# Attention with a threshold, then a token and channel mixer: fewer weight conversions in two units, and a second layer for two tiles in turn

## The chip, the cores and the metric

The kernel runs on one core of one Trainium2 chip. The metric is device time in microseconds (us). The kernel before took 1351.52 us in the median of three runs, from 1350.7 to 1352.07. The engines of the core are named as in the profile: PE is TensorE (matrix multiplications; PEld are its weight loads), DVE is VectorE, ACT is ScalarE, POOL is GpSimd, and SP is SyncE, which here only starts transfers. A name with q behind it (SPq, ACTq) is the queue in which that engine issues its transfers.

## The reference

For 8 batches of 8 heads, 576 tokens and 64 values a head, each row of scores is cut at a threshold below its maximum, and what is left goes through a softmax. The heads are then put side by side to 512 channels, and a mixer follows: two layers over the tokens (576 to 256 to 576) with a sum, and two layers over the channels (512 to 1536 to 512) with a sum.

```python
scores = scale * np.matmul(q, k.transpose(0, 1, 3, 2))
thresh = np.max(scores, axis=-1, keepdims=True) - tau
scores = np.where(scores >= thresh, scores, -1000000000.0)
scores = scores - np.max(scores, axis=-1, keepdims=True)
attn = np.exp(scores)
attn = attn / (np.sum(attn, axis=-1, keepdims=True) + 1e-09)
attn_out = np.matmul(attn, v)
# ... heads side by side: x is (8, 576, 512)
h = np.maximum(xt @ w_tok1, 0.0) @ w_tok2       # xt: x with tokens last
u = x + h.transpose(0, 2, 1)
h2 = np.maximum(u @ w_ch1, 0.0) @ w_ch2
return u + h2
```

The four weight matrices come as 64-bit floating-point numbers. [...] the kernel takes them apart as integer words and puts 32-bit numbers together: this is what is called conversion below.

## The kernel before

The program is one loop over 144 *units*. A unit is 128 rows of scores for the two heads of a pair; 18 units are one batch, called a row here (units 0 to 17 are row 0, units 18 to 35 are row 1). The instructions of each engine run in the order in which the loop writes them down.

Softmax of a unit: TensorE computes the scores of both heads into two banks, VectorE takes the row maxima, GpSimd makes the bias from them, ScalarE subtracts, cuts and exponentiates, GpSimd divides by the sums. From row 1 on two banks serve all units, so the scores of a unit wait until ScalarE's first activation (`Prelu`) has read those of the unit before.

```python
def scores(u):
    # ...
    nc.tensor.matmul(sc[h][rows, f, 0:HS], lhsT=qT[r, cols], rhs=kT[r, HS * f : HS * f + HS], start=True, stop=True)
    # ...
    nc.vector.tensor_reduce(out=mx[:, c], in_=sc[h][:, :, 0:HS], axis=AX.XY, op=ALU.max)
    nc.gpsimd.tensor_scalar(out=bias[:, c], in0=mx[:, c], scalar1=toff, scalar2=-SCALE, op0=ALU.add, op1=ALU.mult)

def weigh(u):
    # ...
    nc.scalar.activation(out=eh, in_=sc[h][:, :, 0:HS], func=AF.Prelu, bias=bias[:, h : h + 1], scale=SCALE, alpha=STEEP)
    # ...
    nc.scalar.activation(out=eh, in_=eh, func=AF.Exp, bias=ntau, accum_out=rs[:, h : h + 1])
```

Two units later the weights are transposed (*turned*) for the product with the values. In row 0 this is done on TensorE, into two banks that VectorE and ScalarE empty in turn (`turn`). From row 1 on it is done in 32 by 32 blocks on VectorE, and every third unit SyncE issues 16 transfers that put the blocks in place (`turn_blocks`). The first two units of row 1, 18 and 19, still turn the last two units of row 0.

```python
def turn(u, third):
    # ...
    on = nc.scalar.copy if third == 1 else nc.vector.tensor_copy
    on(out=eTs[key][:, 3 * third : 3 * third + 3, P * place : P * place + P], in_=ps)

def turn_blocks(u):
    # ...
    nc.vector.transpose(
        out=T[:, :, place, :].rearrange("p a (c x) -> p c a x", c=NK), in_=e.rearrange("p (c a x) -> p c a x", c=NK, a=4)
    )
    if place == GU - 1:
        # ...
        for a in range(4):
            for i in range(4):
                nc.sync.dma_start(out=eT[32 * a : 32 * a + 32, :, i, :], in_=T[32 * i : 32 * i + 32, a, :, :])
```

The conversion: 31 pieces (0 to 2 and 3 to 6 for the two token layers, 7 to 18 for the first channel layer, 19 to 30 for the second), three steps each, and step number k is part k mod 3 of piece k div 3. Part 0 lets GpSimd finish the piece before and then loads a raw piece three ahead into one of four raw buffers, in SyncE's queue; parts 1 and 2 are ScalarE's two operations on the *next* piece; every part has one of VectorE's three operations. `need` runs all steps up to one that a matmul needs.

```python
def weight(n):
    for k in range(steps_done, min(steps_done + n, 3 * len(pieces) + 1)):
        i, part = divmod(k, 3)
        if part == 0:
            on_gpsimd(i - 1)
            if i:
                load_piece(i - 1 + NRAW)
        else:
            on_scalar(i + 1, part - 1)
        on_vector(i, part)
        steps_done = k + 1

def need(i):
    weight(3 * i + 4 - steps_done)
```

The mixer's matmuls are steps in a list, `todo`, each with a cost. `fill` takes them from it and places them between the units. For a group of 256 tokens, the first channel layer is 12 steps (`ch1`), and the second, for each of two tiles of 128 tokens, four parts of three matmuls that sum into one bank (`ch2`). The pool `ps_mm` has two banks.

```python
def ch2(t, part):
    need(7 + NJ + 3 * part + 2)
    # ...
    if part == 0:
        s["ps"] = ps_mm.tile([P, NCC, P], F32, tag="mm", name=f"c2_{b}_{i}_{t}")
    ps = s["ps"]
    # ... three matmuls into ps; after part 3 the bank goes to SBUF and out
```

The loop, cut to the order of its parts (`turns_left` holds in units 18 and 19 alone):

```python
turns_left = b_now and back and not in_blocks(units[w][0])
scores(u)
# ... values of row 0
norm(u - 1)
if b_now:
    if turns_left:
        weigh(u)
    else:
        weight(2)
# ... copies; turns on TensorE
if b_now:
    fill(0.4)
if back and in_blocks(wb):
    turn_blocks(w)
if b_now:
    weight(4 if turns_left else 2)
if turns_left:
    fill(0.6)
elif on and (b_now or not visit):
    weigh(u)
# ...
if b_now:
    weight(2)
# ... loads and block transposes of q and k for later pairs; values
```

Of the kernel before, what the change touches and what calls it, by code (L numbers as in the profile page):

```python
# [9 lines left out]
F32 = mybir.dt.float32  # L10
# [7 lines left out]
P = 128  # L18
# [3 lines left out]
def kernel(  # L22
# [38 lines left out]
    NCC = DM // P  # L61
# [16 lines left out]
    ps_mm = None  # L78
# [98 lines left out]
    def load_piece(i):  # L177
        if i >= len(pieces):
            return
        dst, src = pieces[i]  # L180
        rows = dst.shape[0]
        n = 1
        for d in dst.shape[1:]:
            n *= d
        raw = raw_at[i % NRAW][0:rows, 0 : n * (2 if wide(i) else 1)].bitcast(src.dtype)
        nc.sync.dma_start(out=like(raw, dst), in_=src)
        if wide(i):
            words = raw.bitcast(U32).rearrange("p (n w) -> p n w", w=2)
            h2 = high[0:rows, WMAX * (i % 2) : WMAX * (i % 2) + n]
            raws[i] = like(words[:, :, 0], dst), like(words[:, :, 1], dst), like(h2, dst)  # L190
        else:
            raws[i] = like(raw, dst)
# [4 lines left out]
    def on_scalar(i, part):  # L197
        if wide(i):
            lo, hi, h2 = raws[i]
            if part == 0:  # L200
                nc.scalar.activation(out=lo.bitcast(I32), in_=lo, func=AF.Copy, scale=2.0**-29)
            else:
                nc.scalar.activation(out=h2, in_=hi.bitcast(F32), func=AF.Abs)
# [17 lines left out]
    def on_gpsimd(i):  # L221
        if i >= 0:
            dst = pieces[i][0]
            if wide(i):
                nc.gpsimd.tensor_tensor(out=dst.bitcast(I32), in0=dst.bitcast(I32), in1=raws.pop(i)[0].bitcast(I32), op=ALU.add)
            else:
                nc.gpsimd.tensor_copy(out=dst, in_=raws.pop(i))
# [5 lines left out]
    def weight(n):  # L233

        nonlocal steps_done
# [10 lines that stand above are left out]
# [5 lines left out]
    def need(i):  # L251

        weight(3 * i + 4 - steps_done)
# [27 lines left out]
    def in_blocks(b):  # L281
        return b > 0
# [201 lines left out]
    def channel_mlp(b, uT, i):  # L484

        s = {}
        n = min(GR, 2 * S - GR * i)
        nt = n // P

        def turn_u():  # L490

            us, ut = s["us"], s["ut"]
            nc.vector.transpose(
                out=us[:, 0:nt].rearrange("q n a (c d) -> q c (n a) d", c=NCC),
                in_=uT[:, :, GR * i : GR * i + n].rearrange("q c (m r) -> q c m r", r=32),
            )

            def move(a, k):
                nc.sync.dma_start(out=ut[32 * a : 32 * a + 32, 0:nt, k, :], in_=us[32 * k : 32 * k + 32, 0:nt, a, :])

            moves.extend([lambda a=a, k=k: move(a, k) for a in range(4) for k in range(4)])

        def ch1(j):
            need(7 + j)
            if j == 0:
                s["g"] = work.tile([P, NJ, GR], F32, tag="g", bufs=1, name=f"g_{b}_{i}")
            ps = ps_mm.tile([P, GR], F32, tag="mm", name=f"c1_{b}_{i}_{j}")[:, 0:n]
            for c in range(NCC):
                nc.tensor.matmul(ps, lhsT=wc1[:, j, c, :], rhs=uT[:, c, GR * i : GR * i + n], start=(c == 0), stop=(c == NCC - 1))  # L509
            nc.scalar.activation(out=s["g"][:, j, 0:n], in_=ps, func=AF.Relu)  # L510
            if j == 1:
                s["us"] = work.tile([P, GR // P, 4, NCC * 32], F32, tag="us", bufs=1, name=f"us_{b}_{i}")
                if b:
                    s["ut"] = work.tile([P, GR // P, 4, NCC * 32], F32, tag="ut", bufs=1, name=f"ut_{b}_{i}")
                    turn_u()

        def ch2(t, part):
            need(7 + NJ + 3 * part + 2)
            t0 = GR * i + P * t
            if part == 0:  # L520
                s["ps"] = ps_mm.tile([P, NCC, P], F32, tag="mm", name=f"c2_{b}_{i}_{t}")
            ps = s["ps"]
            flat = ps.rearrange("q c d -> q (c d)")
            if part == 0 and not b:
                for c in range(NCC):
                    nc.tensor.matmul(
                        ps[:, c, :], lhsT=uT[:, c, t0 : t0 + P], rhs=ident, is_transpose=True, start=(c == 0), stop=False, skip_group_check=True
                    )
            for j in range(3 * part, 3 * part + 3):
                nc.tensor.matmul(  # L530
                    flat,
                    lhsT=s["g"][:, j, P * t : P * t + P],
                    rhs=wc2[:, j, :],
                    start=(j == 0 and b > 0),
                    stop=(j == NJ - 1),
                    skip_group_check=True,
                )
            if part == 3:
                o = s["us"][:, t].rearrange("q a x -> q (a x)")
                if b:  # L540
                    move_u()
                    nc.vector.tensor_add(  # L542
                        out=o.rearrange("q (c k d) -> q c k d", c=NCC, k=4),
                        in0=ps.rearrange("q c (k d) -> q c k d", k=4),
                        in1=s["ut"][:, t].rearrange("q k (c d) -> q c k d", c=NCC),
                    )
                else:
                    nc.vector.tensor_copy(out=o, in_=flat)
                nc.sync.dma_start(out=out[b : b + 2].rearrange("b s d -> (b s) d")[t0 : t0 + P, :], in_=o)

        def ch2_last(half):

            t0 = GR * i
            w = DM // 2
            ps = ps_mm.tile([P, w], F32, tag="mm", name=f"c2_{b}_{i}_h{half}")
            for j in range(NJ):
                nc.tensor.matmul(  # L557
                    ps, lhsT=s["g"][:, j, 0:P], rhs=wc2[:, j, w * half : w * half + w], start=(j == 0), stop=(j == NJ - 1)
                )
            if half == 0:  # L560
                move_u()
            o = s["us"][:, half].rearrange("q a x -> q (a x)")[:, 0:w]
            cs = slice(NCC // 2 * half, NCC // 2 * half + NCC // 2)
            nc.vector.tensor_add(
                out=o.rearrange("q (c k d) -> q c k d", c=NCC // 2, k=4),
                in0=ps.rearrange("q (c k d) -> q c k d", c=NCC // 2, k=4),
                in1=s["ut"][:, 0].rearrange("q k (c d) -> q c k d", c=NCC)[:, cs],
            )
            nc.sync.dma_start(out=out[b : b + 2].rearrange("b s d -> (b s) d")[t0 : t0 + P, w * half : w * half + w], in_=o)

        if b == B - 2 and n == P:
            return [(0.0067 * n, lambda j=j: ch1(j)) for j in range(NJ)] + [(5.2, lambda half=half: ch2_last(half)) for half in range(2)]
        return [(0.0067 * n, lambda j=j: ch1(j)) for j in range(NJ)] + [
            (2.6 if part or b else 3.0, lambda t=t, part=part: ch2(t, part)) for t in range(nt) for part in range(4)
        ]

    def move_u():
        while moves:
            moves.popleft()()
# [56 lines left out]
    def values_due(u):  # L636
        while due and due[0][0] <= u:
            _, b, p0, g = due.popleft()
            values(b, p0, g)
            if b == 0 and p0 == 0 and g == 2:  # L640
                return True
            if p0 == NP - 2 and g == 2:
                if not in_blocks(b):
                    return True
                push(b)
        return False

    for u in range(len(units) + LAG + 4):
        on = u < len(units)
        if u == UB:  # L650
            late.close()
            ps_mm = ctx.enter_context(tc.tile_pool(name="ps_mm", bufs=2, space=bass.MemoryType.PSUM))
        if on:
            b_now, p0, t = units[u]
# [6 lines left out]
        last = False  # L661
        visit = False
        if due and not in_blocks(due[0][1]):
            visit = due[0][0] <= u
            last = values_due(u)
# [6 lines left out]
        turns_left = b_now and back and not in_blocks(units[w][0])  # L672
# [29 lines left out]
        if back and in_blocks(wb):  # L702
            turn_blocks(w)
        if b_now:
            weight(4 if turns_left else 2)
        if turns_left:
            fill(0.6)
        elif on and (b_now or not visit):
# [62 lines left out]
```

## Time and profile before

| what | before |
| --- | --- |
| median of three runs | 1351.52 us (1350.7 to 1352.07) |
| span of the profiled run | 1349.9 us |
| busy: PE, DVE, ACT, POOL | 1306.6, 592.2, 585.1, 352.5 us |
| chain that ended last, PE's share | 86% |
| chain, DVE's share and that of transfers | 6% and 3% |
| one maximum on DVE (L311) | 750 ns |
| one block transpose on DVE (L369) | 1364 ns |
| one first activation on ACT (L321) | 739 ns |
| raw weight load (512 KB), issue to landing | 3.7 us |

The rows of the page are groups of instructions with the same line of the program: L306 scores, L311 maxima, L312 bias, L321 and L328 the activations, L357 and L359 the turns of row 0 and the copies out of their banks, L369 the block transposes and L378 their transfers, L201 and L203 ScalarE's conversion operations, L211, L213 and L217 those of VectorE, L225 that of GpSimd, L186 the raw loads, L413 and L418 the products with the values, L425 the copies of these, L456 and L466 the token layers, L470 the sums behind them, L509 and L510 the first channel layer, L526 and L530 the second. The chain of waits is the work that ended last, followed back from the end: what is not in it did not set the time. The slices give the busy share of each engine in 40 equal parts of the span, some 34 us each. A timeline line has start, length, engine, line, operation, and in brackets the idle time before it and what ended it. The clock column, PEclk, is the share of full speed that TensorE was granted.

### The profile page before, as it was taken

How to read it: one execution, taken by the hardware profiler on the slowest of the kernel's cores; microseconds unless marked ns; L12 is line 12 of the kernel's file. 1: busy time of each engine (PE TensorE's matmuls, PEld its weight loads, DVE VectorE, ACT ScalarE, POOL GpSimd, SP SyncE). 2: the span in 40 equal slices, each digit the busy share in tenths (PEclk: the TensorE clock that was granted, in tenths of full speed). 3: DMA queues.
4: the chain of work that ended last, by engine and by line, in shares of the span. 5: the costliest groups of instructions: out<-in, count | busy, mean ns of one | idle time of the engine just before them, and what ended most of it. 6: DMA issues, size and time to landing. Idle time of an engine off the chain costs nothing.

```text
span 1349.9 us, 17890 instructions
## 1 busy us (share of the span) xinstructions
PE 1306.6 (97%) x6186; PEld 817.1 (61%) x6186; DVE 592.2 (44%) x1026; ACT 585.1 (43%) x1299; POOL 352.5 (26%) x683
## 2 busy tenths in 40 slices
PE   7888899999999999999999999999999999999999
PEld 5565556547474666655665567565656566575677
DVE  6878874445443435434334445434443454201000
ACT  6777654444445435443434444354333454120110
POOL 4565652222222213222222222222221222100000
PEclk8998999999999999999999999999999999999999
DMA  5535764535353544543345435535443453400000
GB/s 123 120 87 127 199 168 97 127 94 136 83 133 89 114 109 96 126 109 88 86 107 125 98 85 123 125 82 115 109 102 83 114 118 79 112 22 17 23 24 32
DMA packets 296746, 135.31 MB, mean 100 GB/s; under 512 B 204816, under 2 KB 289552, under 8 KB 296656
## 3 DMA queue, kind: packets, MB, share of 16 engines
q1 hardware_dynamic: 168944, 118.27, 34.4%
q10 hardware_dynamic: 127712, 15.90, 7.4%
q8 instruction: 49, 0.80, 0.3%
q14 instruction: 41, 0.34, 0.1%
HBM read 43.25 MB, written 9.44 MB: 39 GB/s over the span
## 4 chain that ended last, share of the span: by engine, by line
PE 86%; DVE 6%; DMA 3%; ACT 2%; SPq 1%; issue 1%; POOL 1%; ACTq 0%; DVEq 0%; POOLq 0%
PE c L530 26%; PE c L509 26%; PE sc L306 11%; PE pv L418 9%; PE t L456 5%; PE t L466 4%; PE pv L413 3%; DVE mx L311 2%; PE tx L449 1%; DMA lk<-in_k_dram 1%; ACT e L321 1%; SPq L378 1%; PE c_h L557 1%; DVE T L369 1%; DVE high L211 1%
## 5 line engine op out<-in xcount | busy, mean ns | idle before, releaser
L509 PE MATMUL c<-xT,wc 128*128 128x256 f32 (+1 forms) x1920 | 400.1, 362 | 0.1
L311 DVE TENSOR_REDUCE mx<-sc 128x1 f32<-128x576 f32 x288 | 204.4, 750 | 444.3 <-PE sc L306 443.2
L530 PE MATMUL c<-wc,g 128*128 128x512 f32 x840 | 379.0, 597 | 0.0
L509 PEld LDWEIGHTS c<-xT,wc 128*128 128x128 f32 x1920 | 334.9, 191 | 69.3 <-issue 29.7
L312 POOL TENSOR_SCALAR bias<-mx,toff 128x1 f32<-128x1 f32 x288 | 81.1, 282 | 775.6 <-DVE mx L311 722.7
L321 ACT ACTIVATE e<-sc,bias 128x576 f32<-128x576 f32 x288 | 199.8, 739 | 182.5 <-POOL bias L312 176.7
L530 PEld LDWEIGHTS c<-wc,g 128*128 128x128 f32 x840 | 154.7, 190 | 176.1 <-issue 172.4
L328 ACT ACTIVATE e<-e,ntau 128x576 f32<-128x576 f32 x288 | 221.1, 771 | 0.0
L339 POOL TENSOR_SCALAR e<-e,rr 128x576 f32<-128x576 f32 x288 | 214.3, 756 | 14.8 <-ACT g L510 2.6
L510 ACT ACTIVATE g<-c 128x256 f32<-128x256 f32 (+1 forms) x240 | 86.7, 361 | 296.5 <-PE c L509 283.4
L306 PE MATMUL sc<-kT,qT 64*128 64x288 f32 (+1 forms) x1280 | 190.3, 433 | 6.9 <-ACT e L321 5.9
L369 DVE STREAM_TRANSPOSE T<-e 128x1152 f32<-128x1152 f32 x126 | 171.9, 1364 | 5.5 <-DMA eT<-T 2.9
L306 PEld LDWEIGHTS sc<-kT,qT 64*128 64x128 f32 (+1 forms) x1280 | 105.2, 178 | 92.2 <-issue 57.2
L418 PE MATMUL pv<-eT,lv 128*64 128x384 f32 (+1 forms) x1024 | 136.8, 408 | 0.0
L418 PEld LDWEIGHTS pv<-eT,lv 128*64 128x64 f32 x1024 | 76.9, 138 | 49.9 <-issue 42.1
L423 ACT COPY xT<-pv 128x384 f32<-128x384 f32 (+1 forms) x56 | 21.0, 400 | 164.6 <-PE pv L418 159.5
L466 PE MATMUL t<-w,a 128*128 128x288 f32 x256 | 75.2, 421 | 8.2 <-DVE xT L470 4.8
L542 DVE TENSOR_TENSOR us<-c,ut 128x512 f32<-128x512 f32 x26 | 17.9, 690 | 137.5 <-PE c L530 122.7
L456 PE MATMUL t<-x_sb,w 128*128 128x512 f32 (+1 forms) x180 | 72.4, 549 | 0.0
L466 PEld LDWEIGHTS t<-w,a 128*128 128x128 f32 x256 | 45.9, 192 | 30.2 <-issue 10.5
L470 DVE TENSOR_TENSOR xT<-xT,t 128x288 f32<-128x288 f32 x64 | 28.3, 446 | 70.6 <-PE t L466 69.9
L328 ACT ACTIVATION_READ_ACCUMULATOR e<-e,ntau 128x1 f32 x288 | 56.7, 197 | 0.0
(51 smaller groups left out, 571.2 us busy)
## 6 DMA issues: line engine op xcount, KB each, us to landing
eT<-T SPq DMA_DIRECT2D x672, 108.0 KB, 2.3
scratch<-in_moe_w_ch_dram SPq DMA_DIRECT2D x24, 512.0 KB, 3.7
lv<-in_v_dram SPq DMA_DIRECT2D x32, 288.0 KB, 3.5
out_dram<-us SPq DMA_DIRECT2D x35, 256.0 KB, 2.2
lk<-in_k_dram ACTq DMA_DIRECT2D x109, 72.0 KB, 2.7
lq<-in_q_dram ACTq DMA_DIRECT2D x106, 72.0 KB, 2.3
ut<-us SPq DMA_DIRECT2D x192, 32.0 KB, 1.9
lk<-in_k_dram SPq DMA_DIRECT2D x19, 72.0 KB, 3.2
```

The source lines that it names most:

```text
L306: nc.tensor.matmul(sc[h][rows, f, 0:HS], lhsT=qT[r, cols], rhs=kT[r, HS * f : HS * f + HS], start=True, stop=True)
L311: nc.vector.tensor_reduce(out=mx[:, c], in_=sc[h][:, :, 0:HS], axis=AX.XY, op=ALU.max)
L321: nc.scalar.activation(out=eh, in_=sc[h][:, :, 0:HS], func=AF.Prelu, bias=bias[:, h : h + 1], scale=SCALE, alpha=STEEP)
L328: nc.scalar.activation(out=eh, in_=eh, func=AF.Exp, bias=ntau, accum_out=rs[:, h : h + 1])
L339: nc.gpsimd.tensor_scalar(out=eh, in0=eh, scalar1=rr[:, h : h + 1], scalar2=1.0, op0=ALU.mult, op1=ALU.mult)
L369: nc.vector.transpose(out=T[:, :, place, :].rearrange("p a (c x) -> p c a x", c=NK), in_=e.rearrange("p (c a x) -> p c a x", c=NK, a=4))
L418: nc.tensor.matmul(to[r], lhsT=lv[:, j, :], rhs=e[j], start=False, stop=(c == NI - 1), skip_group_check=True)
L456: nc.tensor.matmul(to, lhsT=w1[:, t, P * m : P * m + P], rhs=x_sb[:, t, cols], start=(t == 0), stop=(t == NT - 1))
L466: nc.tensor.matmul(to, lhsT=a[:, m, P * c : P * c + P], rhs=w2[:, m, HS * f : HS * f + HS], start=(m == 0), stop=(m == NTK - 1))
L509: nc.tensor.matmul(ps, lhsT=wc1[:, j, c, :], rhs=uT[:, c, GR * i : GR * i + n], start=(c == 0), stop=(c == NCC - 1))
L510: nc.scalar.activation(out=s["g"][:, j, 0:n], in_=ps, func=AF.Relu)
L530: nc.tensor.matmul(flat, lhsT=s["g"][:, j, P * t : P * t + P], rhs=wc2[:, j, :], start=(j == 0 and b > 0), stop=(j == NJ - 1), skip_group_ ...
```

## The change

In units 18 and 19, which have turns of row 0 left, the loop ran six conversion steps each, four between the fills and two at the end; now it runs only the two at the end. VectorE is to come sooner to the copies that free the banks of the turns. What is not converted there is converted later, so the last steps move to a later unit. So that the second channel layer does not ask for its last pieces too early and force their conversion in one go, its parts are put in another order for the first group of tokens: part 0 of both tiles, then part 1 of both, and so on. Each tile then needs a bank of its own, kept under the tile's number.

```diff
             if part == 0:
-                s["ps"] = ps_mm.tile([P, NCC, P], F32, tag="mm", name=f"c2_{b}_{i}_{t}")
-            ps = s["ps"]
+                s[t] = ps_mm.tile([P, NCC, P], F32, tag="mm", name=f"c2_{b}_{i}_{t}")
+            ps = s[t]
@@
+        last = [(t, part) for t in range(nt) for part in range(4)]
+        if b == 0 and i == 0:
+            last.sort(key=lambda x: x[1])
         return [(0.0067 * n, lambda j=j: ch1(j)) for j in range(NJ)] + [
-            (2.6 if part or b else 3.0, lambda t=t, part=part: ch2(t, part)) for t in range(nt) for part in range(4)
+            (2.6 if part or b else 3.0, lambda t=t, part=part: ch2(t, part)) for t, part in last
         ]
@@
         if b_now:
-            weight(4 if turns_left else 2)
+            weight(0 if turns_left else 2)
         if turns_left:
             fill(0.6)
```

## The prediction

> **What bounds the kernel now.** I read the page's busy times and slices first, then busy times by stretch, then the timeline of each engine in the stretch that the change touches, and last the chain of waits there.
>
> ```profile
> PE 1306.6 (97%) x6186; PEld 817.1 (61%) x6186; DVE 592.2 (44%) x1026; ACT 585.1 (43%) x1299; POOL 352.5 (26%) x683
> ...
> PE   7888899999999999999999999999999999999999
> ...
> DVE  6878874445443435434334445434443454201000
> ```
>
> TensorE sets the time: only 43 us of the span is without a matmul, and most of it lies in the first five slices (170 us), where VectorE is at 7 to 8 tenths. There every unit has a softmax and weight conversions, and TensorE waits for it. So the change can win only idle time before about 190 us. Beyond that, every microsecond by which TensorE is moved is carried to the end, because its order is fixed in the program.
>
> The timeline of TensorE, 92 to 166 us (start, length, operation, in brackets the wait and its releaser). Scores of units 18 to 26 start at 98.53, 103.58, 112.11, 126.13, 131.43, 142.84, 149.39, 159.48 and 166.66; in the later timeline units 27, 28 and 30 start at 174.13, 185.45 and 196.98.
>
> ```profile
> 103.58 1.51 PE L306 MATMUL sc<-kT,qT 64*128 64x288 f32 x8
> ...
> 111.28 0.90 PE L357 MATMUL tr<-ident,e 128*128 128x128 f32 x3 [4.37 <-DVE eT L359]
> 112.11 2.29 PE L306 MATMUL sc<-kT,qT 64*128 64x288 f32 x8
> ...
> 138.41 2.29 PE L466 MATMUL t<-w,a 128*128 128x288 f32 x4 [3.02 <-DVE xT L470]
> ...
> 149.39 1.24 PE L306 MATMUL sc<-kT,qT 64*128 64x288 f32 x8
> ...
> 159.48 1.86 PE L306 MATMUL sc<-kT,qT 64*128 64x288 f32 x8 [1.82 <-ACT e L321]
> ```
>
> The wait of 4.37 us is the one the change aims at: the third transpose of unit 19 needs a bank that VectorE empties only after its six conversion steps of unit 18 (104.17 to 108.80 us) and the row maxima. A second cost follows it in the clock column (busy times by stretch: sum, PE, PEld, DVE, ACT, POOL, PEclk, DMA share, GB/s):
>
> ```profile
> 111.00:117.00 6.00, 5.72 (x21) 2.74 (x23) 4.87 (x8) 4.39 (x10) 4.03 (x4) 0.50 0.36 98
> ```
>
> Six microseconds at half clock: scores of 2.29 us that take 1.24 elsewhere. Now the part of the stretch that I think decides the case, on the queue of SyncE (first fence) and on ScalarE (second):
>
> ```profile
> 140.90 10.55 SPq L378 DMA_DIRECT2D eT<-T  x16
> 151.57 5.36 SPq L186 DMA_DIRECT2D scratch<-in_moe_w_ch_dram  x4
> ```
>
> ```profile
> 155.41 0.69 ACT L201 ACTIVATE scratch<-scratch 128x512 int32<-128x512 uint32 x1 [5.08 <-DMA scratch<-in_moe_w_ch_dram]
> ...
> 182.24 0.68 ACT L201 ACTIVATE scratch<-scratch 128x512 int32<-128x512 uint32 x1 [6.20 <-DMA scratch<-in_moe_w_ch_dram]
> ```
>
> Every third unit (22, 25, 28) sends 16 block moves, 0.66 us of issue each, 10.55 us together. A weight load that stands behind them in the queue is issued only then, and lands 3.8 us later. ScalarE, whose conversion step needs it, stands still meanwhile, with all that follows it in order. The chain of waits goes through exactly this:
>
> ```profile
> 141.44 0.17 SPq L378
> ...
> 151.57 3.82 DMA scratch<-in_moe_w_ch_dram
> 155.41 0.33 ACT scratch L201
> ```
>
> **What the Trainium skill says.** "TensorE: Matmul & The Clock Gate", section "What's actually happening": after an idle window of about 3.4 us the array runs at half rate, until about 3.4 us of sustained work. The trace agrees in kind: 4.37 us and 3.02 us idle are each followed by a clock of 0.50 (until 117.3 and 141.4 us), 1.82 us idle is not; the release took 6 us and 3 us here. "DMA: Bandwidth & Descriptors", section "Anatomy of one DMA — SWDGE (gpsimd) path": a wait is served on the issuing sequencer before dispatch, so what is behind it in that queue is held; the SyncE queue shows it (52.8 us of L186 waiting for GpSimd between 96 and 200 us). "SBUF — State Buffer", section "Terms": VectorE and GpSimd share a port pair as an exclusive lock: L213 takes 0.44 us alone and 1.40 us beside L225, so a conversion step on VectorE costs 0.42 to 1.5 us, 0.73 in the mean of 58 (42.6 us in all), and which of the two it is depends on alignment.
>
> **The change, part by part.** No instruction is added or taken away; the engines' totals stay. I followed the step counter through both programs. Before: steps 36 to 41 in unit 18, 42 to 47 in unit 19, then six a unit, the last (93) in unit 27. After: 36 and 37 in unit 18, 38 and 39 in unit 19, then six a unit, 93 in unit 28. So each conversion comes 8 steps (one unit and a third) later, and each raw weight load with it.
>
> *Gain in units 18 to 20.* After the bank copy that ends at 104.25, VectorE has two steps (0.9 us) instead of 4.6 us; the maxima of unit 19 start at 105.1 (its scores end there) instead of 108.72, the bank of unit 19 is copied at about 107.3, the third transpose starts at 107.9 instead of 111.28. The idle time falls from 4.37 to about 1.0 us, so the clock stays full. Scores 20 follow at 108.7 and the values at about 110.8, after ScalarE's bank copy (its four activations of unit 19 end near 110.3): another 0.9 us of wait that was hidden before. Values (3.4), the token products (3.2), transposes and first token layer (4.0) bring scores 21 to about 121.3, against 126.13: **4.8 us gained** (estimate from these rows: 3.4 us of idle time and 3.0 us of slow clock, less 0.9 and less 0.7 of small waits).
>
> *Units 21 and 22.* No gain here: from unit 20 on there are six steps a unit as before. VectorE needs 7.84 us in unit 21 (127.67 to 135.51) where TensorE has 5, so the 3.02 us wait and its clock dip stay, only 4.8 us earlier. The block transpose that ended at 140.01 ends at about 135.2.
>
> *Loss in units 23 and 24.* This follows from the order of instructions in the changed program. Before, the first load behind the moves of unit 22 is that of piece 24 (step 63); ScalarE uses it at step 70, in the last steps of unit 23, after that unit's activations `e`. After, it is piece 21 (step 54), used at step 61, ahead of the activations of unit 23. Scores 24 need the two banks that these activations free. So: moves from 135.3 to 145.8 (the 0.9 us in front of them before was a load that waited for GpSimd, which is now elsewhere), load issued 145.9, landed 149.7, step 0.6, first activation 0.74: scores 24 at about 151.1. TensorE is through with unit 23 at 149.39 less 4.8, that is 144.6. It idles 6.5 us, and then runs cold, about 3 us lost as at 111. Unit 24 has 8.2 us of matmuls (1.2 scores, 3.5 values, 3.5 first layer): scores 25 at 151.1 + 8.2 + 3.0 = 162.3, against 159.48. The 1.82 us wait there is gone, and the kernel is already 2.8 us behind.
>
> *Loss in units 26 and 27.* The same again with the moves of unit 25. Before, piece 30 is caught (used in the last steps of unit 26, the 6.20 us wait above), which cost TensorE 0.94 us at scores 28. After, it is piece 27 (step 72, used at step 79), ahead of the activations of unit 26. Maxima 25 at 163.6, block transpose done 3.8 us later, 167.4; moves to 177.9; landed 181.8; scores 27 at 183.1 against 174.13, and TensorE, which needs 13.1 us for units 25 and 26, is ready at 175.4: 7.7 us idle, then 3 us of slow clock. Unit 27 with its values is 10.9 us: scores 28 at 197.0 against 185.45, **11.5 us late**.
>
> *Unit 28 and the order of the second layer.* Six steps more in unit 28 make VectorE's part 7.8 us against TensorE's 4.1, but unit 29 has 7 us of matmuls, so scores 30 stand at about the same distance; I take 0 to 0.5 us off. Taking the two tiles in turn changes no matmul and no count. It holds both banks of the pool from unit 27 to unit 31, while nothing else asks for one; without it the need of step 76 and later ones would force conversions in a burst in units 27 and 28. Its own effect: 0.
>
> Sum: −4.8 + 7.6 + 8.7 = +11.5 at unit 28, about +11 at unit 30, carried to the end: 1351.5 + 11, shaded to 1361 for the rivals.
>
> **The rivals.**
> 1. *The gain alone.* If ScalarE is not held at unit 23 (the block transposes come earlier because VectorE has fewer steps behind it, or the load lands sooner), the first wait and its cold clock go and nothing returns: −5 to −7 us, 1345 to 1347. For it: it is what the change is for, and the wait of 4.37 us is plainly VectorE's. Against it: VectorE reaches maxima 21 without a backlog in both kernels (127.67 against scores that end at 127.37), so the moves shift no more than TensorE does, and the order of the loads in the queue is fixed.
> 2. *A wash.* Only one of the two stalls happens, or the slow clock costs less than 3 us: −5 + 6 to 8, 1351 to 1356. For it: a stall of 6.5 us may be cut where some matmuls of the next unit stand in front of scores.
> 3. *Worse.* Both stalls, and VectorE falls behind in units 24 and 27, since its step on piece 21 or 27 stands behind ScalarE's second half, which comes after the late activations: 2 to 4 us more, 1364 to 1367.
>
> **Range and chances.** I give the two stalls 75% (1357 to 1367), the wash 12%, the gain 13%. Predicted 1361 us, range 1352 to 1367. 2% are 27 us in either direction, several times the gain on one side, and more than twice the predicted loss on the other: faster 0.01, within 2% 0.96, slower 0.03.
>
> **What would show it.** Right: the wait for the bank in unit 19 near 1 us and no 0.50 in the clock from 108 to 117 us; a wait of TensorE's scores for `e` of some 6 us near 145 to 151 us and of 8 us near 175 to 183; ScalarE waits of 8 to 10 us for `scratch` just ahead of these, each behind 16 moves; clock 0.50 after each. Wrong: scores 24 less than 8.5 us after scores 23; or no wait of more than 3 us on TensorE after 140 us, in which case the time is below 1350; or the loss shows in units 28 to 31 instead, which would put it on the longer tail of conversions or on the two tiles taken in turn.

## The result, and the profile after

The changed kernel took 1362.93 us in the median of six runs (1360.96 to 1364.94), the kernel before 1352.44 us beside it (1350.7 to 1354.7). The ratio is 1.0077, with a 95% interval from 1.0063 to 1.0091: slower by 0.8%, or 10.5 us. The prediction was 1361.

The page of the changed kernel, busy times and two rows of the slices:

```profile
PE 1311.6 (96%) x6186; PEld 819.8 (60%) x6186; DVE 587.4 (43%) x1026; ACT 584.9 (43%) x1299; POOL 355.2 (26%) x683
...
PE   7888879999999999999999999999999999999999
...
PEclk7999889999999999999999999999999999999999
```

The same number of instructions on each engine, and nearly the same busy times. TensorE has a 7 in the sixth slice (170 to 204 us) where it had a 9, and its clock an 8 in the fifth and sixth where it had a 9: idle time and slow clock between 136 and 204 us. The timeline of TensorE (start, length, operation, wait and releaser), to be read beside the lines of the kernel before in the prediction:

```profile
106.49 1.51 PE L306 MATMUL sc<-kT,qT 64*128 64x288 f32 x8
...
110.45 0.55 PE L357 MATMUL tr<-ident,e 128*128 128x128 f32 x3 [0.62 <-DVE eT L359]
110.93 1.24 PE L306 MATMUL sc<-kT,qT 64*128 64x288 f32 x8
...
135.41 2.29 PE L466 MATMUL t<-w,a 128*128 128x288 f32 x4 [2.73 <-DVE xT L470]
...
142.18 5.45 PE L509 MATMUL c<-xT,wc 128*128 128x256 f32 x24
152.91 2.91 PE L306 MATMUL sc<-kT,qT 64*128 64x288 f32 x8 [5.29 <-ACT e L321]
...
172.24 5.45 PE L509 MATMUL c<-xT,wc 128*128 128x256 f32 x24
184.83 2.92 PE L306 MATMUL sc<-kT,qT 64*128 64x288 f32 x8 [7.14 <-ACT e L321]
```

The wait for the bank in unit 19 is 0.62 us instead of 4.37, and scores 20 run at full speed. That is the gain. Then scores 24 and 27 wait 5.29 and 7.14 us for ScalarE's activations `e`, and run for 2.9 us instead of 1.24. In the kernel before they did not wait; scores 27 there:

```profile
174.13 1.24 PE L306 MATMUL sc<-kT,qT 64*128 64x288 f32 x8
```

The clock (seventh value after the stretch) had fallen:

```profile
151.00:157.00 6.00, 4.09 (x11) 2.87 (x12) 0.87 (x2) 5.42 (x12) 0.10 (x1) 0.51 0.82 277
...
184.00:190.00 6.00, 5.17 (x16) 3.42 (x17) 1.93 (x6) 6.00 (x14) 0.37 (x2) 0.61 0.90 262
```

What held ScalarE is seen in the queue of SyncE (first lines) and on ScalarE (second): each time 16 moves, a raw load behind them, and a conversion step that waits for that load and stands directly in front of the activations.

```profile
137.04 10.90 SPq L378 DMA_DIRECT2D eT<-T  x16
148.05 16.71 SPq L186 DMA_DIRECT2D scratch<-in_moe_w_ch_dram  x6
169.25 10.31 SPq L378 DMA_DIRECT2D eT<-T  x16
179.68 1.01 SPq L186 DMA_DIRECT2D scratch<-in_moe_w_ch_dram  x2
```

```profile
151.58 0.65 ACT L201 ACTIVATE scratch<-scratch 128x512 int32<-128x512 uint32 x1 [6.99 <-DMA scratch<-in_moe_w_ch_dram]
152.14 1.35 ACT L321 ACTIVATE e<-sc,bias 128x576 f32<-128x576 f32 x2
...
183.50 0.65 ACT L201 ACTIVATE scratch<-scratch 128x512 int32<-128x512 uint32 x1 [8.73 <-DMA scratch<-in_moe_w_ch_dram]
184.05 1.35 ACT L321 ACTIVATE e<-sc,bias 128x576 f32<-128x576 f32 x2
```

The chain of waits of the changed kernel runs through these links without a gap (start, length, what; the second stall):

```profile
178.96 0.60 SPq L378
...
179.68 3.73 DMA scratch<-in_moe_w_ch_dram
183.50 0.65 ACT scratch L201
...
184.15 0.64 ACT e L321
...
184.83 2.92 PE sc L306 x7
```

The times from the start of one unit's scores to that of another's show in which units the time went. They leave out what lies ahead of unit 19, where the profiles start up to 3 us apart (unit 19 starts at 103.58 us before and 106.49 after, with the same instructions in front of both).

| scores | before | after | difference | predicted |
| --- | --- | --- | --- | --- |
| 19 to 21 | 22.55 | 16.02 | −6.5 | −4.8 |
| 21 to 23 | 16.71 | 18.50 | +1.8 | 0 |
| 23 to 25 | 16.64 | 22.85 | +6.2 | +7.6 |
| 25 to 28 | 25.97 | 33.87 | +7.9 | +8.7 |
| 28 to 30 | 11.53 | 10.67 | −0.9 | −0.5 to 0 |
| sum | 93.40 | 101.91 | +8.5 | +11 |

The spans of the two profiles are 12.4 us apart: 2.9 ahead of scores 19, 8.5 here and 1.0 after scores 30. The 2.9 are not the change's: over all fourteen profiles unit 19 starts between 102.89 and 106.57 us.

### The profile page after: what moved, and what is told of

The parts are those of the page before. It is cut to its first block, busy times and chain, and to the rows that moved or that the text cites. A ratio compares the mean times of both kernels' runs of the same rounds, so it can differ in the third digit from the quotient of the medians.

```text
span 1362.3 us, 17888 instructions
## 1 busy us (share of the span) xinstructions
PE 1311.6 (96%) x6186; PEld 819.8 (60%) x6186; DVE 587.4 (43%) x1026; ACT 584.9 (43%) x1299; POOL 355.2 (26%) x683
## 4 chain that ended last, share of the span: by engine, by line
PE 87%; DVE 4%; DMA 3%; ACT 3%; SPq 2%; issue 1%; POOL 1%; ACTq 0%; DVEq 0%; POOLq 0%
PE c L509 26%; PE c L530 26%; PE sc L306 11%; PE pv L418 9%; PE t L456 5%; PE t L466 4%; PE pv L413 3%; DVE mx L311 2%; SPq L378 2%; DMA lk<-in_k_dram 1%; PE tx L449 1%; ACT e L321 1%; PE tr L357 1%; PE c_h L557 1%; ACT e L328 1%
## 5 line engine op out<-in xcount | busy, mean ns | idle before, releaser
L339 POOL TENSOR_SCALAR e<-e,rr 128x576 f32<-128x576 f32 x288 | 217.0, 766 | 14.1 <-ACT g L510 2.6
L306 PE MATMUL sc<-kT,qT 64*128 64x288 f32 (+1 forms) x1280 | 193.7, 439 | 16.6 <-ACT e L321 14.4
L466 PEld LDWEIGHTS t<-w,a 128*128 128x128 f32 x256 | 45.8, 192 | 31.0 <-issue 10.5
```

Of the source, the lines that this page charges most:

```text
L339: nc.gpsimd.tensor_scalar(out=eh, in0=eh, scalar1=rr[:, h : h + 1], scalar2=1.0, op0=ALU.mult, op1=ALU.mult)
L466: nc.tensor.matmul(to, lhsT=a[:, m, P * c : P * c + P], rhs=w2[:, m, HS * f : HS * f + HS], start=(m == 0), stop=(m == NTK - 1))
```

## The experiments

The theory was that of the prediction: a raw load written behind the moves is late by the length of the moves, and it costs TensorE much only if the step that uses it stands ahead of a unit's activations. Loads are written every third step, a unit has six steps, and the moves come every third unit, so which load is caught depends on the step counter modulo three. Rivals: conversions that come later cost by themselves (the tail in unit 28), the two tiles in turn cost something, or the moves fill the transfer engines, so that any load is late then.

### One more step, and nothing else

The kernel before, with seven steps in unit 18. All later steps come one earlier; the counter modulo three is then that of the changed kernel.

```diff
-            weight(4 if turns_left else 2)
+            weight((5 if u == UB else 4) if turns_left else 2)
```

> The kernel before, with seven conversion steps instead of six in unit 18, so that every later step comes one earlier. Theory (the place of a late weight load in ScalarE's order): the step counter then stands as in the changed kernel modulo three; the first loads behind the block moves of units 22 and 25 are used ahead of the activations of units 23 and 26, both stalls come, 1359 to 1364 us, although less is left to convert. Rival (the later conversions and the tail in unit 28 are the loss): nothing is later here, 1351 to 1354 us. Rival (the two tiles in turn): they are not here, 1351 to 1354 us.

Measured: 1370.48 us, ratio 1.0123 (1.0108 to 1.0138). TensorE in this kernel:

```profile
114.62 0.90 PE L357 MATMUL tr<-ident,e 128*128 128x128 f32 x3 [4.71 <-DVE eT L359]
...
160.44 2.91 PE L306 MATMUL sc<-kT,qT 64*128 64x288 f32 x8 [5.99 <-ACT e L321]
...
191.98 2.91 PE L306 MATMUL sc<-kT,qT 64*128 64x288 f32 x8 [7.05 <-ACT e L321]
```

Both large waits are there, of about the same size as in the changed kernel, with nothing converted later and no tiles in turn. The first two rivals fall as causes of them. The size that I expected was wrong: I had taken the net loss of the change, but here nothing is gained in unit 19 (4.71 us of wait), so the whole cost shows: +17.3 us, of which 15.3 lie between scores 19 and 30. Each against the kernel before beside it, that is 6.8 us more than the changed kernel lost, which is about the 6.5 us gained there.

### The step counter, from three to seven later

The changed kernel with other numbers of steps in units 18 and 19, five kernels with one of these lines each:

```diff
-            weight(0 if turns_left else 2)
+            weight(1 if turns_left else 2)                            # three and three: six later
+            weight((1 if u == UB else 4) if turns_left else 2)        # or: three and six: three later
+            weight((0 if u == UB else 4) if turns_left else 2)        # or: two and six: four later
+            weight((1 if u == UB else 2) if turns_left else 2)        # or: three and four: five later
+            weight((1 if u == UB else 0) if turns_left else 2)        # or: three and two: seven later
```

> The changed kernel, with three steps instead of two in units 18 and 19, so that later steps come six later than before, not eight. Theory: the counter modulo three is that of the kernel before, the late loads are used behind the activations, the stalls shrink to those of before (TensorE waits of 1 to 2 us), and the gain in units 19 and 20 remains: 1345 to 1350 us. Rival (later conversions and the tail in unit 28): still six steps later, three quarters of the loss stays, 1358 to 1361 us. Rival (tiles in turn): kept, 1360 us or more.

> The changed kernel with three steps in unit 18 and six in unit 19, so that later steps come three later than before. Theory (the step counter modulo three decides whether a late load is used ahead of the activations or behind them): 3 is the same as 0, no large stall. The wait in unit 19 goes, and only three steps are left for unit 28, so the tail that took back the gain with six later steps is shorter: 1346 to 1351 us. Rival (what matters is how much is converted later): on the line between 0 and 8 steps, 1355 to 1358 us.

> The changed kernel with two steps in unit 18 and six in unit 19: four later. Theory: 4 modulo three is 1; the loads are then written in the first and third pair of a unit and used in the third pair of the next, behind the activations: no large stall, 1346 to 1351 us. Rival (how much is later): 1356 to 1359 us.

> The changed kernel with three steps in unit 18 and four in unit 19: five later. Theory: 5 modulo three is 2, as 8 and -1 are; both stalls come: 1358 to 1364 us, some 8 to 12 us above the kernels with four and six later steps, between which it lies. Rival (how much is later, or the tail): 1352 to 1356 us, between its neighbours.

> The changed kernel with three steps in unit 18 and two in unit 19: seven later, one less than the change. Theory: 7 modulo three is 1, no large stall; the gain stays until unit 27 and the tail takes most of it back, as with six: 1350 to 1354 us, 8 us and more below the changed kernel for one step. Rival (how much is later): 1360 to 1362 us.

All results of this kind, in the order of the counter (each ratio is to the kernel before on the same chip):

| steps later | modulo 3 | median us | ratio, 95% interval |
| --- | --- | --- | --- |
| −1 | 2 | 1370.48 | 1.0123 (1.0108 to 1.0138) |
| 3 | 0 | 1351.32 | 0.9999 (0.9988 to 1.0009) |
| 4 | 1 | 1352.38 | 1.0006 (0.9996 to 1.0017) |
| 5 | 2 | 1363.25 | 1.0093 (1.0078 to 1.0108) |
| 6 | 0 | 1351.71 | 0.9988 (0.9981 to 0.9995) |
| 7 | 1 | 1352.22 | 1.0006 (0.9997 to 1.0014) |
| 8, the change | 2 | 1362.93 | 1.0077 (1.0063 to 1.0091) |

Five is slower than four and six on either side, and eight than seven, by some 10 us and more. An amount converted later can't do that; the place of the loads can. TensorE with five later, and then with seven:

```profile
152.03 2.92 PE L306 MATMUL sc<-kT,qT 64*128 64x288 f32 x8 [5.88 <-ACT e L321]
...
185.97 2.92 PE L306 MATMUL sc<-kT,qT 64*128 64x288 f32 x8 [8.11 <-ACT e L321]
```

```profile
153.70 2.34 PE L306 MATMUL sc<-kT,qT 64*128 64x288 f32 x8 [1.79 <-ACT e L321]
...
182.06 1.86 PE L306 MATMUL sc<-kT,qT 64*128 64x288 f32 x8 [0.97 <-ACT e L321]
```

With seven, these are scores 25 and 28, and 24 and 27 don't wait.

What I missed is the gain: I expected up to 6 us from the kernels without stalls, and the best of them, with six later, is faster by 0.12%. With three, four and six later the medians lie 0.3, 1.4 and 1.7 us above what I expected. With six later the gain is there up to scores 24: from scores 19 it takes 38.47 us against 45.81 before. ScalarE and TensorE after that (six later):

```profile
150.10 0.69 ACT L201 ACTIVATE scratch<-scratch 128x512 int32<-128x512 uint32 x1 [6.83 <-DMA scratch<-in_moe_w_ch_dram]
...
177.05 0.69 ACT L201 ACTIVATE scratch<-scratch 128x512 int32<-128x512 uint32 x1 [6.22 <-DMA scratch<-in_moe_w_ch_dram]
...
181.54 0.67 ACT L201 ACTIVATE scratch<-scratch 128x512 int32<-128x512 uint32 x1 [3.21 <-DMA scratch<-in_moe_w_ch_dram]
```

```profile
153.84 2.56 PE L306 MATMUL sc<-kT,qT 64*128 64x288 f32 x8 [2.29 <-ACT e L321]
...
183.44 1.86 PE L306 MATMUL sc<-kT,qT 64*128 64x288 f32 x8 [2.78 <-ACT e L321]
185.23 4.54 PE L530 MATMUL c<-wc,g 128*128 128x512 f32 x6
```

The chain of moves and load does not get shorter; TensorE meets it at scores 25, where 5.3 of the 7.3 us gained are left. The wait at 177.05 is the counterpart of that at 182.24 before. The one at 181.54 has none, because before the load caught there was the last of all: it is for a piece that is converted later, whose load stands behind the same moves. It costs scores 28 a wait and a stretch of slow clock (six matmuls in 4.54 us, 2.84 in the changed kernel), and from 25 to 30 this kernel takes 42.38 us against 37.50. With three, four and seven later it is 42.23, 38.82 and 39.81. So the tail of late conversions does cost, 1.3 to 4.9 us, where the stalls do not hide it. But the cost does not grow with the number of steps: three later lose 4.7 us and six 4.9, four lose 1.3 and seven 2.3. It goes by the counter modulo three as well, which speaks for the place of the last loads and not for their number. That was not tried by itself: it would take a kernel that converts the last pieces elsewhere. With seven later 3.1 us of the gain are left at scores 30, and 1.9 of these go right after it, where the values wait 1.83 us for the moves of unit 28.

### Each half of the change alone

> The changed kernel with six steps again in units 18 and 19: only the order of the second layer's parts for the two tiles is changed. Theory: no effect, 1351 to 1354 us. Rival (the two banks held at once cost time): above 1356 us.

The edit is the change without its last hunk. Measured: 1353.03 us, ratio 0.9997 (0.9987 to 1.0006). The two tiles in turn cost nothing by themselves.

> The kernel before with two steps instead of six in units 18 and 19 and the old order of the second layer. Theory: all of the loss is here, 1361 to 1365 us, the same as the changed kernel; no conversion is forced, as the counter is at 84 when step 76 is asked for. The prediction said that without the new order conversions would be forced in a burst: then 1364 us or more. Rival (tiles in turn are the loss): 1347 to 1350 us.

The edit is the last hunk of the change alone. Measured: 1364.23 us, ratio 1.0079 (1.0064 to 1.0094), so the loss is here. No conversion is forced: the steps run in the same order on VectorE as in the changed kernel. The old order of parts has another cost, which is seen in unit 29 alone (TensorE):

```profile
202.13 1.12 PE L530 MATMUL c<-wc,g 128*128 128x512 f32 x2 [0.36 <-POOL wc L225]
...
204.55 1.12 PE L530 MATMUL c<-wc,g 128*128 128x512 f32 x2 [1.30 <-POOL wc L225]
```

The matmuls reach pieces that GpSimd has not finished: 1.66 us. The new order avoids this, but the total of the two kernels does not tell them apart.

### The loads out from behind the moves

The second pair of steps ahead of the block transpose, so that the loads of pieces 21 and 27 are issued ahead of the moves:

```diff
+        ahead = b_now == 1 and not turns_left
+        if ahead:
+            weight(2)
         if back and in_blocks(wb):
             turn_blocks(w)
-        if b_now:
+        if b_now and not ahead:
             weight(0 if turns_left else 2)
```

> The changed kernel, with the second pair of steps of each unit of row 1 from unit 20 on written ahead of the block transpose and its moves, so that the loads of pieces 21 and 27 are issued before the 16 moves. Theory (a load behind the moves, used ahead of the activations): the next late loads are pieces 22 and 28, used in the first steps of units 24 and 27, behind the activations of 23 and 26: no wait of TensorE's scores 24 and 27 above 2 us, smaller ones at 25 and 28, as with three steps a unit: 1349 to 1354 us. Rival (later conversions themselves): 1360 us or more.

Measured: 1357.81 us, ratio 1.0042 (1.0027 to 1.0057), 3.8 us above what I expected. On TensorE:

```profile
169.12 1.86 PE L306 MATMUL sc<-kT,qT 64*128 64x288 f32 x8 [0.21 <-ACT e L321]
183.63 2.04 PE L306 MATMUL sc<-kT,qT 64*128 64x288 f32 x8 [2.90 <-ACT e L321]
...
205.15 1.07 PE L413 MATMUL pv<-eT,vl 128*64 128x384 f32 x4 [2.19 <-DMA eT<-T]
```

Scores 24 do not wait and scores 27 wait 0.21 us: from 19 to 27 this kernel takes 66.23 us against 70.55 before, so 4.3 us of the gain are left. They are lost after that, at scores 28 (2.90 us) and in unit 30, where the values wait for the moves of unit 28. These now stand behind two more steps; that this is the reason was not tried.

The same two loads from another queue:

```diff
-        nc.sync.dma_start(out=like(raw, dst), in_=src)
+        (nc.gpsimd if i in (21, 27) else nc.sync).dma_start(out=like(raw, dst), in_=src)
```

> The changed kernel, in which two of the 31 raw loads, those of pieces 21 and 27, are issued from GpSimd's queue instead of SyncE's, where they stood behind the moves. Nothing else is different. Theory: these two loads alone hold ScalarE in units 23 and 26, so both large waits go and 1349 to 1355 us are left, with some wait passed on to pieces 22 and 28, which still stand behind the moves. Rival (the moves fill the transfer engines, so any load is late then): waits stay above 4 us, 1359 us or more.

Measured: 1355.38 us, ratio 1.0022 (1.001 to 1.0034), just above what I expected. Scores 24 do not wait, scores 27 wait 2.78 us. Two transfers out of 31 make up 7 of the 10 us. They are not free: the 16 moves of unit 22 took 13.96 us beside the first of them instead of 10.90.

All loads from piece 20 on in that queue (`i >= 20` in the same line), in the changed kernel and in the one before:

> The changed kernel with the loads of pieces 20 to 30 issued from GpSimd's queue, none of them behind the moves. Theory: no wait of ScalarE for a raw load above 3 us in units 23 to 28, and the gain of units 19 and 20 stays: 1344 to 1349 us. If GpSimd pays more than 1 us of issue for a load, 1348 to 1352 us. Rival (later conversions): 1360 us or more.

> The kernel before with the loads of pieces 20 to 30 issued from GpSimd's queue. Theory: its waits of 5.08 and 6.20 us of ScalarE go, which cost TensorE 1.82 and 0.94 us: 1349 to 1352 us; the wait of 4.37 us in unit 19 stays. Against the kernel with the change and the same queue it is then 3 to 6 us slower: with the loads out of the way, the change would do what it was meant to.

Measured: 1362.58 us, ratio 1.007 (1.0053 to 1.0088), and 1359.6 us, ratio 1.0048 (1.0031 to 1.0065). Both miss by far. SyncE's queue in the changed kernel of the two:

```profile
136.91 16.09 SPq L378 DMA_DIRECT2D eT<-T  x16
```

TensorE in the other:

```profile
163.35 1.55 PE L413 MATMUL pv<-eT,vl 128*64 128x384 f32 x4 [5.59 <-DMA eT<-T]
```

And the transfers by kind between 96 and 210 us in the changed kernel (count, size, median us to landing):

```profile
scratch<-in_moe_w_ch_dram POOLq DMA_DIRECT2D x11, 512.0 KB, 5.8
eT<-T SPq DMA_DIRECT2D x47, 108.0 KB, 3.0
scratch<-in_moe_w_ch_dram SPq DMA_DIRECT2D x6, 512.0 KB, 3.6
```

The waits for `e` at 24 are gone, but now the 16 moves take 16.09 us instead of 10.90, and the values of unit 24, which need them, hold TensorE: for 5.59 us in the kernel before with these loads, for 5.93 us in the changed one. (In the changed one the profile puts this wait down to a load of q, which the values do not read; the last moves, issued at 152.4, landed up to 5.8 us later, which fits the end of the wait at 158.27.) So the third rival is half right. Behind the moves, a load waits for its turn in the queue; beside them, both get slower. In one queue the late party is the conversion, in two it is the values.

## Why the prediction was right

*The bank in unit 19.* Right, and too small: 6.5 us gained between scores 19 and 21 against 4.8 predicted. The wait was 0.62 us, not 1.0, and of the small waits that I had added in unit 20 (0.9 and 0.7) 0.17 us came; another one, of 0.24, was there before.

*Units 21 and 22.* Here a step failed: "No gain here", and no loss, was off by 1.8 us. The 2.73 us wait stayed as predicted, but 0.70 us of wait came ahead of it, and the cold clock after it held longer (eight matmuls of the first layer took 3.58 us, 2.42 before). Five and eight later both show the 0.70 us, six and seven do not.

*The two stalls.* Right in place and cause, as the shift by one, five and eight steps against four, six and seven shows. They were a little smaller than predicted: waits of 5.29 and 7.14 us for 6.5 and 7.7, ScalarE held 6.99 and 8.73 us for "8 to 10". Together with the slow clock 14.1 us for 16.3.

*The clock.* The prediction read that 3.02 us of idle time were followed by slow clock and 1.82 us were not. That slow clock would follow both stalls held. But no boundary by length comes out of the traces: the clock fell to 0.50 after waits of 1.69 us (six later, at 95.73) and 1.88 us (the changed kernel, at 98.94), and stayed at 1.00 after 2.88 us (seven later, at 132.79) and 3.03 us (six later, at 132.31). So a difference of 1 to 2 us between two kernels may be the clock alone.

*The tiles in turn.* Right that their own effect is 0, by the run of that half alone. But the reason for it, in the prediction and where the change is described, was wrong: without the new order nothing is forced. The counter stands at 84 when step 76 is asked for. What the new order avoids is a wait of 1.66 us for GpSimd.

*The tail.* The prediction gave it 0 to 0.5 us off, and in the changed kernel it was 0.9 off: there the tail cost nothing. As a general statement it would have been wrong: a part of the gain is lost there in each of the four kernels without stalls.

*The sum.* +8.5 between scores 19 and 30 against +11 predicted: a gain too small by 1.7, a missed loss of 1.8, and stalls too large by 2.2, with 0.5 or so at unit 28. The medians are 10.5 us apart, the prediction said 9.5. Which waits come was foreseen; that the sum came so close is partly luck, since a missed gain and a missed loss of some 1.8 us each cancelled.

*The rivals.* "The gain alone" and "a wash" do not hold for the change itself. For the kernels with the counter elsewhere it is the wash that happens, and for a reason that the prediction did not give: the gain meets the chain of moves and loads at scores 25, and most of what was left is lost by scores 30 (with seven later, by 32).

## What to carry to other kernels

When work is shifted in a program with a fixed order, follow each transfer that goes with it: what it stands behind in its queue, and what stands behind the instruction that waits for it. Here 10 us hung on whether that instruction came ahead of a unit's activations or behind them, which repeated with every third step. And a wait that is removed brings time only up to the next chain that does not get shorter with it: the four kernels with the counter elsewhere ended within 0.12% of the kernel before, whatever they had gained at unit 19.

## What the runs showed of the hardware

The 16 moves of 108 KB took SyncE's queue longer the more was loaded from other queues meanwhile: 10.31 us with nothing issued there (unit 25 of the changed kernel), 10.90 us with two loads of 72 KB from ScalarE's queue (unit 22), 11.95 us with four of these (the loads ahead of the moves), 13.96 us with four of these and one raw load of 512 KB from GpSimd's queue, and 16.09 us with four of each. In this last case one move landed 4.9 us after its issue in the median, 2.2 us in unit 22 of the changed kernel; the raw loads from GpSimd's queue between 96 and 210 us landed in 5.8 us in the median, those of the changed kernel from SyncE's queue in 3.7. I had expected a second queue to take the loads out of the way. What exactly the transfers share was not tried.
